# Turning the mixed input of batches 3 and 4 on VectorE, with a trip through DRAM, instead of on TensorE

## The chip, the cores and the metric

One core of a Trainium2 chip runs the whole program. The metric is the device time of one execution in microseconds; three executions of the kernel before took 647.86, 649.02 and 649.75 us (median 649.02). The engines are named as the profile names them: PE (TensorE, the matrix products; PEld is its loading of the stationary operand), DVE (VectorE), ACT (ScalarE), POOL (GpSimd) and SP (SyncE, which here only issues DMA transfers). "Line" numbers (L699) are those of the kernel before, and behind the change those of the changed kernel.

## The reference

Four batches of 768 tokens go through an attention (8 heads of 64; local window and block summaries), and its output x (768 x 512) through a mixing block:

```python
def _moe_ref(x, U, V, w_ch1, w_ch2):
    xt = x.transpose(0, 2, 1)
    h = xt @ U @ V                       # low rank mix over the tokens, rank 32
    u = x + h.transpose(0, 2, 1)         # the "mixed input"
    ch = np.maximum(u @ w_ch1, 0.0) @ w_ch2
    return (u + ch).astype(np.float32)
```

with w_ch1 of 512 x 2048 and w_ch2 of 2048 x 512. Queries and keys are drawn eight times as wide as the values.

## The kernel before, in words

Batches are numbered 1 to 4 in this text and 0 to 3 in the code (`st.b`). The program is one hand-written order of instructions for each engine; every engine works through its own in order, and waits on semaphores where an operand or a buffer isn't ready. SP's order is the DMA queue: a transfer whose source isn't ready holds those behind it.

*Stages.* Batch 1's attention comes first. Then batch 1's two large products run while batch 2's attention is slipped in between. For batches 2, 3 and 4 there is an **up phase** (u times w_ch1, by a seven-product scheme for 2 x 2 blocks, with operands B11 to T4 made ahead of it) and a **down phase** (times w_ch2). While batch b is in its two phases, batch b + 1's attention and its operands are slipped in: `later_steps` lists 32 steps and 8 calls of `operands`; the first 15 go with the up phase, the other 25 are spread evenly over the down phase, so about one for every 3.6 of its 96 output tiles. Batch 2's phases thus carry batch 3's steps, batch 3's carry batch 4's, and batch 4's carry none.

*Down phase.* For each of 16 slices f of the hidden layer there are six output tiles, four of 128 x 512 (three products each) and two of pairs of 128 x 256 (six products). The hidden values of a slice become a high part gh (ACT, L1284) and a rest gl (DVE, L1288), called a **gate** here. ACT's half for slice f + 1 is issued at the first tile of slice f, DVE's after its second. Six PSUM banks hold the output, two are left for everything else.

*Mixed input.* The attention writes x with tokens on the partitions (`st.x`, six token tiles u by 512 channels). The products want channels on the partitions. `operands(st, i, k)` does this for one channel tile c = 2i + k % 2 and one half of the tokens (hf = 1 for k = 0 and 1, else 0): `mix_u` turns three 128 x 128 blocks with an identity (L699) into a bank and adds the low rank part h in the same bank by one product (L707). From that bank ACT keeps the value in place of x (`keep`, L735, read again at the end of the batch) and makes the high part of a B operand (L738); DVE makes differences T1 to T4 with values kept earlier (L752) and the rests (L742, some on POOL). The calls are i = 0, k = 0 to 3, then i = 1, k = 0 to 3, the last four near the end of the down phase; k = 0 only keeps.

*Squares.* The attention weights of batches 3 and 4 already go a way like the new one: DVE turns 32 x 32 squares (L430), SP sends them to DRAM (L435), and fetches them sorted (L443); `value products` (L490) use them.

*Places.* `hidden_place(k)` are eight SBUF buffers h0 to h7, which hold the hidden values of slices 2k and 2k + 1 during the down phase. `val` is a ring of eight small buffers for differences, loads and outputs. `prepare` splits weights into high and low parts on ACT and POOL (L179, L180), `fetch_weight` loads them (L884).

Of the kernel before, what the change touches and what calls it, by code (L numbers as in the profile page):

```python
# [10 lines left out]
F32 = mybir.dt.float32  # L11
F32R = mybir.dt.float32r
AF = mybir.ActivationFunctionType
ALU = mybir.AluOpType
# [4 lines left out]
P = 128  # L19
BLOCK, WIN = 32, 16  # L20
NB = S // BLOCK
NU = S // P
# [12 lines left out]
NH = S // 2  # L35
# [45 lines left out]
def f32(ap):  # L81
    return ap.bitcast(F32)
# [3 lines left out]
def body(ctx: ExitStack, tc, q0, q1, k, v, vn, uv, w1, w2, mask, ident, rep, out):  # L86
    nc = tc.nc
# [10 lines left out]
    def bank(name):  # L98
        return psum.tile([P, 512], F32, name=name, tag="bank")
# [16 lines left out]
    def hidden_place(k, dt=F32):  # L116
        return wt.tile([P, 4 * NH], dt, name="place", tag=f"h{k}")
# [68 lines left out]
    def new_batch(b):  # L186
        st = Batch()
        st.b = b
        st.qt, st.kt, st.km, st.vt, st.vn, st.vsum, st.neg = ({} for _ in range(7))
        st.e, st.at, st.psx, st.t4, st.u = ({} for _ in range(5))  # L190
        st.op, st.tmp, st.h = ({} for _ in range(3))
        st.ps_s, st.ps_t, st.ps_m, st.ps_r, st.ps_u, st.ps_n = ({} for _ in range(6))
        return st

# [243 lines left out]
    def fetch_squares(st, h):  # L438
# [3 lines left out]
        for j in range(4):  # L442
            nc.sync.dma_start(  # L443
                out=at[32 * j : 32 * j + 32].rearrange("k i u q -> k i (u q)"), in_=there[j]
            )

    def turn_half(st, h, a):

        transposes(st, h, a)
        ps = st.ps_t.pop((h, a))  # L450
        if a == 0:
            st.at[h] = att.tile([P, 4, NU, 32], F32, name="at", tag=("at", "squares")[h % 2], bufs=1)
        at = st.at[h][:KC, :, 3 * a : 3 * a + 3].rearrange("k i u q -> k u i q")
        nc.scalar.copy(at, ps[:KC, : 3 * P].rearrange("k (u i q) -> k u i q", i=4, q=32))
# [86 lines left out]

    MIX, BACK = (20, 30), (22, 31)

    def later_step(st, i):

        h, a = divmod(i, 3)
        if i in PRODUCTS:  # L550
            square_values(st, PRODUCTS[i])
            normalise(st, PRODUCTS[i])
        if a == 0:
            if 1 <= h <= H:
                send_squares(st, h - 1)
            if 2 <= h <= H + 1:
                fetch_squares(st, h - 2)
            if h < H:
                scores_by_subtiles(st, h)
                exponentials(st, h, 0)  # L560
            if 3 <= h <= H:
                load_v(st, h - 1)
        elif a == 1:
            if h < H:
                exponentials(st, h, 1)
            if h + 1 < H:
                key_maxima(st, h + 1)
            if 1 <= h <= H:
                for t in range(2):
                    value_summaries(st, h - 1, t, nc.scalar.copy)  # L570
        else:
            if h + 2 < H:
                load_qk(st, h + 2)
            if h == 2:
                st.x = mo.tile([P, NU, DM], F32, name="x")
            if h < H:
                turn_squares(st, h)
        if i in (5, 8):
            load_vsum(st, 1, i // 8)
        if i in (7, 10):  # L580
            slow.append(add_vsum(st, 1, i // 10))
        if i in MIX:
            mix(st, 2 * MIX.index(i))
        if i in BACK:
            mix_back(st, 2 * BACK.index(i))
# [65 lines left out]
    def later_steps(st):  # L651

        todo = [(later_step, st, i) for i in range(STEPS)]
        for n, x in enumerate(operand_steps(st, 0)):
            todo.insert(BACK[0] + 2 + 2 * n, x)
        return todo + operand_steps(st, 1)


# [36 lines left out]
    def mix_u(st, hf, c):  # L695
# [13 lines left out]
        )  # L709
        st.ps_u[hf, c] = ps  # L710

    def mix_u_out(st, hf, c):
        if hf not in st.u:
            st.u[hf] = [
                hidden_place(4 + 2 * hf + i, F32R).rearrange("p (c q) -> p c q", q=NH) for i in range(2)
            ]
        ps = st.ps_u.pop((hf, c))
        uh, ul = st.u[hf]
        nc.scalar.copy(uh[:, c, :], ps[:, :NH])
        nc.vector.tensor_tensor(ul[:, c, :], ps[:, :NH], f32(uh)[:, c, :], ALU.subtract)  # L720


    def operands(st, i, k):

        if not st.op:
            for j, name in enumerate(OPS):
                t = wt.tile([P, 4 * NH], F32R, name="op", tag=f"op{j}")
                st.op[name] = t.rearrange("p (s i q) -> p s i q", s=2, q=NH)
        hf, c = int(k < 2), 2 * i + k % 2
        mix_u(st, hf, c)  # L730
        ps = st.ps_u.pop((hf, c))[:, :NH]
        kept = channel_rows(st, c)[:, 3 * hf : 3 * hf + 3]

        def keep():
            nc.scalar.copy(kept, ps.rearrange("p (u q) -> p u q", q=P))  # L735

        def high(name, val):
            nc.scalar.copy(st.op[name][:, 0, i], val)  # L738

        def low(name, val, engine):  # L740
            t = st.op[name][:, :, i]
            engine.tensor_tensor(t[:, 1], val, f32(t[:, 0]), ALU.subtract)  # L742

        def part(name, val):
            high(name, val)
            low(name, val, nc.gpsimd)

        def tmp():
            return mo.tile([P, DM], F32, name="tmp", tag="val", bufs=VALS)[:, :NH]

        def combine(out, a, b, op):
            nc.vector.tensor_tensor(*(by_tiles(x) for x in (out, a, b)), op)  # L752

        def by_tiles(x):
            return x if len(x.shape) == 3 else x.rearrange("p (u q) -> p u q", q=P)

        if k == 0:
            keep()
            st.tmp["B12"] = kept
            return  # L760
        name = (None, "B22", "B11", "B21")[k]
        high(name, ps)
        keep()
        if k == 1:
            st.tmp["T3"] = tmp()
            combine(st.tmp["T3"], ps, st.tmp["B12"], ALU.subtract)
            low(name, ps, nc.vector)
            part("T3", st.tmp["T3"])
        elif k == 2:
            st.tmp["T1"] = tmp()  # L770
            st.tmp["T2"] = tmp()
            combine(st.tmp["T1"], st.tmp["B12"], ps, ALU.subtract)
            combine(st.tmp["T2"], st.tmp["T3"], ps, ALU.add)
            low(name, ps, nc.vector)
            part("T1", st.tmp["T1"])
            part("T2", st.tmp["T2"])
        else:
            combine(st.tmp["T3"], ps, st.tmp["T2"], ALU.subtract)
            low(name, ps, nc.vector)
            part("T4", st.tmp["T3"])  # L780

    def channel_rows(st, c):

        return st.x[:, :, c * P : (c + 1) * P]
# [197 lines left out]
    st = sts[0]  # L982
# [117 lines left out]
    def do(items):  # L1100
        for f, *args in items:
            f(*args)
# [263 lines left out]
    for b in range(1, B):  # L1366
# [23 lines left out]
        for i, _ in enumerate(down_phase(cur, g)):  # L1390
            do(steps.get(i, ()))
            tick()
            drip()
            if after and i % NU == 0:
                do([(later_start, after, j) for j in {10: (-6,), 11: (-5,), 12: (-4,), 13: (-3, -1), 14: (-2,)}.get(i // NU, ())])
        behind = []


# [91 lines left out]
```

## Time and profile before

| | |
|---|---|
| three executions, median | 649.02 us (647.86 to 649.75) |
| the profiled execution | 648.17 us, span 646.4 us |
| granted TensorE clock | 1.000 |
| busy: PE, DVE, ACT, POOL | 97%, 56%, 55%, 56% of the span |
| DMA traffic | 115.39 MB, mean 179 GB/s |
| down phase of batch 2 (carries batch 3's steps) | about 284.5 to 369.5 us of the span |
| down phase of batch 3 (carries batch 4's steps) | about 432.7 to 517.5 us |

A row of the groups or of a line's instructions gives the engine, the operation, the tiles written and read, and how often; durations are ns of one instruction where three stand together (least, median, greatest). A row of the timeline gives the start and the length in us, and in brackets for how long the engine sat idle before and what ended that. The chain of waits is followed back from the end of the program: each row starts where the one before releases it. A stretch's row has the busy time of PE, PEld, DVE, ACT and POOL, the clock, DMA's share and GB/s. TensorE's products overlap one another, so their pace is read from starts.

### The profile page before, as it was taken

Reading aid. Unit: us, or ns where it says so; the run is one execution under the profiler, and the core shown is the slowest. Engines: PE = TensorE matmul, PEld = TensorE weight load, DVE = VectorE, ACT = ScalarE, POOL = GpSimd, SP = SyncE. Lnnn points to the kernel's source line nnn. Section 1 sums busy time; section 2 is a strip of 40 time slices with the busy share of each in tenths; the row PEclk is TensorE's granted clock in tenths of the full one; section 3 lists DMA queues with packets and bytes.
Section 4 is the critical chain, followed back from the end, with each engine's and each line's share of the span. In section 5 each row is a group of like instructions: output and inputs, shape, how many; then the busy total and the mean of one; then the engine's idle time right before and its main releaser. Section 6 shows DMA issues by size and latency. Waiting matters only on the chain.

```text
span 646.4 us, 14559 instructions
## 1 busy us (share of the span) xinstructions
PE 627.1 (97%) x5528; PEld 563.4 (87%) x5528; DVE 361.7 (56%) x1002; ACT 354.6 (55%) x788; POOL 363.3 (56%) x391
## 2 busy tenths in 40 slices
PE   5879999999999999999999999999999999999997
PEld 4669988888888899998888899998888899998886
DVE  5779767675857596566444645565544522242223
ACT  4756766656663657675453457775453455553321
POOL 3525977965766875862246765771344565653320
PEclk9999999999999999999999999999999999999999
DMA  9897588866675169896628367887431164342002
GB/s 236 223 380 222 160 296 267 229 201 189 214 232 176 46 213 290 243 265 174 180 78 218 113 204 222 258 258 203 144 116 58 60 183 142 115 131 66 32 1 99
DMA packets 68678, 115.39 MB, mean 179 GB/s; under 512 B 6912, under 2 KB 43648, under 8 KB 68608
## 3 DMA queue, kind: packets, MB, share of 16 engines
q1 hardware_dynamic: 68608, 114.45, 58.9%
q8 instruction: 44, 0.72, 0.5%
q14 instruction: 26, 0.21, 0.1%
HBM read 90.31 MB, written 24.12 MB: 177 GB/s over the span
## 4 chain that ended last, share of the span: by engine, by line
PE 87%; DMA 4%; DVE 3%; SPq 2%; ACT 2%; issue 1%; DVEq 0%; ACTq 0%
PE acc L1316 30%; PE ps_h L1215 27%; PE acc L949 10%; PE ps_h L927 9%; PE ps_x L490 3%; PE ps_s L374 2%; PE ps_s L351 2%; DMA place<-in_w 1%; PE ps_t L460 1%; SPq L215 1%; DMA kt<-in_k 1%; PE ps_u L699 1%; DMA place<-in_v 1%; DMA place<-in_q 1%; PE ps_m L665 1%
## 5 line engine op out<-in xcount | busy, mean ns | idle before, releaser
L180 POOL TENSOR_TENSOR parts<-whole,parts 128x512 fp32r<-128x512 f32 (+1 forms) x144 | 182.3, 1273 | 162.9 <-ACT parts L179 153.1
L1316 PE MATMUL acc<-gh,parts 128*128 128x256 f32 (+1 forms) x768 | 198.2, 340 | 0.0
L1215 PE MATMUL ps_h<-op,parts 128*128 128x384 f32 x1008 | 181.7, 337 | 0.1
L1215 PEld LDWEIGHTS ps_h<-op,parts 128*128 128x128 f32 x1008 | 174.3, 188 | 2.7 <-issue 1.1
L1316 PEld LDWEIGHTS acc<-gh,parts 128*128 128x128 f32 x768 | 132.9, 189 | 17.4 <-issue 1.7
L1316 PE MATMUL acc<-gl,parts 128*128 128x256 f32 (+1 forms) x384 | 129.8, 338 | 0.2
L1288 DVE SCALAR_TENSOR_TENSOR gl<-place,gh 128x768 fp32r<-128x768 f32 x48 | 55.3, 1151 | 71.3 <-ACT gh L1284 71.2
L179 ACT CAST parts<-whole 128x512 fp32r<-128x512 f32 (+1 forms) x144 | 83.3, 583 | 3.3 <-DMA whole<-up 1.0
L1316 PEld LDWEIGHTS acc<-gl,parts 128*128 128x128 f32 x384 | 72.8, 189 | 7.5 <-DVE gl L1288 0.8
L410 ACT ACTIVATE e<-e,neg 128x120 f32<-128x120 f32 x144 | 46.5, 386 | 51.4 <-DVE neg L400 46.9
L927 PE MATMUL ps_h<-place 128*128 128x384 f32 x384 | 74.3, 342 | 0.0
L1284 ACT ACTIVATE gh<-place 128x768 fp32r<-128x768 f32 x48 | 40.5, 844 | 57.1 <-PE acc L1316 48.5
L927 PEld LDWEIGHTS ps_h<-place 128*128 128x128 f32 x384 | 66.2, 188 | 1.4 <-issue 0.4
L949 PE MATMUL acc<-place,gh 128*128 128x512 f32 x192 | 67.3, 405 | 0.0
L155 POOL TENSOR_SCALAR val<-place 128x512 f32<-128x512 f32 (+1 forms) x30 | 47.7, 1607 | 25.9 <-ACT place L142 21.4
L180 POOL TENSOR_TENSOR place<-val,place 128x512 fp32r<-128x512 f32 x29 | 38.7, 1357 | 18.3 <-ACT place L179 18.3
L742 POOL TENSOR_TENSOR op<-tmp,op 128x384 fp32r<-128x384 f32 x24 | 26.3, 1108 | 32.9 <-ACT op L738 30.2
L949 PEld LDWEIGHTS acc<-place,gh 128*128 128x128 f32 x192 | 35.9, 188 | 7.6 <-POOL place L180 0.6
L400 DVE CUSTOM_DVE_ANT_0 e<-ps_s,mask_sb 128x120 f32<-128x120 f32 x144 | 32.8, 277 | 11.3 <-PE ps_s L351 5.9
L949 PE MATMUL acc<-place,gl 128*128 128x512 f32 x96 | 37.7, 393 | 0.1
L161 DVE SCALAR_TENSOR_TENSOR val<-place,val 128x512 int32<-128x512 int32 (+1 forms) x33 | 31.7, 965 | 3.3 <-POOL val L155 3.2
L1241 DVE TENSOR_TENSOR place<-place,ps_h 128x384 f32<-128x384 f32 x24 | 13.2, 551 | 36.2 <-PE ps_h L1215 36.2
(113 smaller groups left out, 796.5 us busy)
## 6 DMA issues: line engine op xcount, KB each, us to landing
place<-in_w SPq DMA_DIRECT2D x32, 512.0 KB, 5.6
whole<-up SPq DMA_DIRECT2D x24, 512.0 KB, 4.4
whole<-down SPq DMA_DIRECT2D x24, 512.0 KB, 4.3
whole<-up SPq DMA_DIRECT2D x24, 384.0 KB, 3.4
vt<-in_v SPq DMA_DIRECT2D x48, 146.2 KB, 3.8
kt<-in_k SPq DMA_DIRECT2D x24, 288.0 KB, 5.9
there<-squares SPq DMA_DIRECT2D x16, 384.0 KB, 4.3
at<-there SPq DMA_DIRECT2D x64, 96.0 KB, 3.5
```

The costliest lines, as they stand in the source:

```text
L155: nc.gpsimd.tensor_scalar(f32(bits), f32(hi), 0.0, None, ALU.mult)
L161: lambda lo, hi, bits: nc.vector.scalar_tensor_tensor(bits, lo, 29, bits, ALU.logical_shift_right, ALU.bitwise_or),
L179: nc.scalar.copy(hi, val)
L180: engine.tensor_tensor(lo, val, f32(hi), ALU.subtract)
L400: nc.vector.tensor_tensor_reduce(out=e[:, u, :], in0=ps[:, i * KC : (i + 1) * KC], in1=mask_sb[:, m, :], scale=-SCALE, scalar=BIG, op0=ALU ...
L410: nc.scalar.activation(e[:, u, :], e[:, u, :], AF.Exp, bias=st.neg[h][:, u : u + 1], scale=-1.0,)
L927: nc.tensor.matmul(ps[:, :NH], w_split[0, f][:, c % 2, part_w, c // 2], ut[:, c, :], start=(n == 0), stop=(n == 3 * NC - 1),)
L949: nc.tensor.matmul(acc[t], gt[:, sl], w_split[1, f][:, part_w], start=(first and j == 0), stop=(last and j == 2),)
L1215: nc.tensor.matmul(ps, a[:, sa, i], b[:, sb, i], start=(first and n == 0), stop=(n == 5), skip_group_check=not first,)
L1284: nc.scalar.activation(gh, h, AF.Relu)
L1288: nc.vector.scalar_tensor_tensor(gl, h, 0.0, f32(gh), ALU.max, ALU.subtract)
L1316: nc.tensor.matmul(place, w[:, part_w, c * P : (c + 1) * P], gt[:, q0:q1], start=(f == 0 and i == 0 and j == 0), stop=(f == NF - 1 and j = ...
```

## The change

For batches 3 and 4 (batch 2 keeps the old way) the three blocks are no longer turned by TensorE. For each channel tile c DVE turns all 32 x 32 squares of x's 128 x 768 values (`turn_rows`), SP sends the result to DRAM (`send_rows`, 384 KB) and fetches it in four transfers of 96 KB so that the squares stand where a full transpose has them (`fetch_rows`). The turned tiles stand in h0 and h2, the fetched ones in h1 and h3. `add_rows` then has TensorE make the low rank part alone in a bank, and DVE adds the fetched tile to it, straight into the place in x where the value is kept. ACT's copy for keeping falls away, and the high parts, differences and rests read the kept value from SBUF instead of the bank. Steps 16, 18, 25 and 29 turn tiles 0 to 3, the step behind each sends, and steps 19, 21, 28 and 31 fetch. The first four calls of `operands` stand one place later among the steps, and the first loads of batch 4 (`later_start`, in batch 2's down phase) are issued at slices 7, 9 and 11 instead of 10, 11 and 12.

```diff
--- before.py
+++ after.py
@@ -188,7 +188,7 @@
         st.b = b
         st.qt, st.kt, st.km, st.vt, st.vn, st.vsum, st.neg = ({} for _ in range(7))
         st.e, st.at, st.psx, st.t4, st.u = ({} for _ in range(5))
-        st.op, st.tmp, st.h = ({} for _ in range(3))
+        st.op, st.tmp, st.h, st.rows = ({} for _ in range(4))
         st.ps_s, st.ps_t, st.ps_m, st.ps_r, st.ps_u, st.ps_n = ({} for _ in range(6))
         return st
@@ -444,6 +444,33 @@
                 out=at[32 * j : 32 * j + 32].rearrange("k i u q -> k i (u q)"), in_=there[j]
             )
+    def turn_rows(st, c):
+        if c % 2 == 0:
+            st.turned = hidden_place(c).rearrange("p (n j u q) -> n p j u q", n=2, j=4, q=32)
+        t = st.rows[c] = st.turned[c % 2]
+        src = channel_rows(st, c).rearrange("p u (j k) -> p j u k", k=32)
+        nc.vector.transpose(t, src)
+    def send_rows(st, c):
+        there = dram.tile([P, 4, NU * 32], F32, name="rows")
+        nc.sync.dma_start(out=there, in_=st.rows[c].rearrange("p j u q -> p j (u q)"))
+        st.rows[c] = there
+    def fetch_rows(st, c):
+        if c % 2 == 0:
+            st.sorted = hidden_place(c + 1).rearrange("p (n i u q) -> n p i u q", n=2, i=4, q=32)
+        there = st.rows[c].rearrange("(i k) j c -> j k i c", k=32)
+        t = st.rows[c] = st.sorted[c % 2]
+        for j in range(4):
+            nc.sync.dma_start(
+                out=t[32 * j : 32 * j + 32].rearrange("k i u q -> k i (u q)"), in_=there[j]
+            )
     def turn_half(st, h, a):
         transposes(st, h, a)
@@ -540,6 +567,10 @@
     PRODUCTS = {9: 0, 12: 1, 14: 2, 17: 3, 20: 4, 23: 5, 26: 6, 29: 7}
     MIX, BACK = (20, 30), (22, 31)
+    ROWS = {16: 0, 18: 1, 25: 2, 29: 3}
+    FETCH = {19: 0, 21: 1, 28: 2, 31: 3}
     def later_step(st, i):
@@ -579,6 +610,11 @@
             load_vsum(st, 1, i // 8)
         if i in (7, 10):
             slow.append(add_vsum(st, 1, i // 10))
+        for behind, act in enumerate((turn_rows, send_rows)):
+            if i - behind in ROWS:
+                act(st, ROWS[i - behind])
+        if i in FETCH:
+            fetch_rows(st, FETCH[i])
         if i in MIX:
             mix(st, 2 * MIX.index(i))
         if i in BACK:
@@ -652,7 +688,7 @@
         todo = [(later_step, st, i) for i in range(STEPS)]
         for n, x in enumerate(operand_steps(st, 0)):
-            todo.insert(BACK[0] + 2 + 2 * n, x)
+            todo.insert(BACK[0] + 3 + 2 * n, x)
         return todo + operand_steps(st, 1)
@@ -709,6 +745,19 @@
         )
         st.ps_u[hf, c] = ps
+    def add_rows(st, hf, c, kept):
+        ps = bank("ps_u")
+        nc.tensor.matmul(
+            ps[:, :NH], st.t_st[:, c], vm_st[:, hf * NH : (hf + 1) * NH], start=True, stop=True
+        )
+        nc.vector.tensor_tensor(
+            kept.rearrange("p u (i q) -> p u i q", q=32),
+            ps[:, :NH].rearrange("p (u i q) -> p u i q", i=4, q=32),
+            st.rows[c][:, :, 3 * hf : 3 * hf + 3].rearrange("k i u q -> k u i q"),
+            ALU.add,
+        )
     def mix_u_out(st, hf, c):
         if hf not in st.u:
             st.u[hf] = [
@@ -727,19 +776,26 @@
                 t = wt.tile([P, 4 * NH], F32R, name="op", tag=f"op{j}")
                 st.op[name] = t.rearrange("p (s i q) -> p s i q", s=2, q=NH)
         hf, c = int(k < 2), 2 * i + k % 2
-        mix_u(st, hf, c)
-        ps = st.ps_u.pop((hf, c))[:, :NH]
         kept = channel_rows(st, c)[:, 3 * hf : 3 * hf + 3]
+        if st.b == 1:
+            mix_u(st, hf, c)
+            val = st.ps_u.pop((hf, c))[:, :NH]
+        else:
+            add_rows(st, hf, c, kept)
+            val = kept
         def keep():
-            nc.scalar.copy(kept, ps.rearrange("p (u q) -> p u q", q=P))
+            if st.b == 1:
+                nc.scalar.copy(kept, by_tiles(val))
         def high(name, val):
-            nc.scalar.copy(st.op[name][:, 0, i], val)
+            nc.scalar.copy(by_tiles(st.op[name][:, 0, i]), by_tiles(val))
         def low(name, val, engine):
             t = st.op[name][:, :, i]
-            engine.tensor_tensor(t[:, 1], val, f32(t[:, 0]), ALU.subtract)
+            engine.tensor_tensor(
+                by_tiles(t[:, 1]), by_tiles(val), by_tiles(f32(t[:, 0])), ALU.subtract
+            )
         def part(name, val):
             high(name, val)
@@ -759,24 +815,24 @@
             st.tmp["B12"] = kept
             return
         name = (None, "B22", "B11", "B21")[k]
-        high(name, ps)
+        high(name, val)
         keep()
         if k == 1:
             st.tmp["T3"] = tmp()
-            combine(st.tmp["T3"], ps, st.tmp["B12"], ALU.subtract)
-            low(name, ps, nc.vector)
+            combine(st.tmp["T3"], val, st.tmp["B12"], ALU.subtract)
+            low(name, val, nc.vector)
             part("T3", st.tmp["T3"])
         elif k == 2:
             st.tmp["T1"] = tmp()
             st.tmp["T2"] = tmp()
-            combine(st.tmp["T1"], st.tmp["B12"], ps, ALU.subtract)
-            combine(st.tmp["T2"], st.tmp["T3"], ps, ALU.add)
-            low(name, ps, nc.vector)
+            combine(st.tmp["T1"], st.tmp["B12"], val, ALU.subtract)
+            combine(st.tmp["T2"], st.tmp["T3"], val, ALU.add)
+            low(name, val, nc.vector)
             part("T1", st.tmp["T1"])
             part("T2", st.tmp["T2"])
         else:
-            combine(st.tmp["T3"], ps, st.tmp["T2"], ALU.subtract)
-            low(name, ps, nc.vector)
+            combine(st.tmp["T3"], val, st.tmp["T2"], ALU.subtract)
+            low(name, val, nc.vector)
             part("T4", st.tmp["T3"])
     def channel_rows(st, c):
@@ -1392,7 +1448,7 @@
             tick()
             drip()
             if after and i % NU == 0:
-                do([(later_start, after, j) for j in {10: (-6,), 11: (-5,), 12: (-4,), 13: (-3, -1), 14: (-2,)}.get(i // NU, ())])
+                do([(later_start, after, j) for j in {7: (-6,), 9: (-5,), 11: (-4,), 13: (-3, -1), 14: (-2,)}.get(i // NU, ())])
         behind = []
```

How the order of each engine's instructions changes is shown at three places of batch 2's down phase, near its end, where batch 3's last four calls of `operands` stand; the names are those of the code, with a buffer's number in some.

TensorE at call k = 2 (acc: the down phase's output; ps_u: the bank of the mixed input). Before:

```order
L1316 MATMUL acc_4093<-gh,parts 128x256 x2
L1316 MATMUL acc_4093<-gl,parts 128x256
L1316 MATMUL acc_4093<-gh,parts 128x256
L699 MATMUL ps_u<-ident_sb,x 128x128 x3
L707 MATMUL ps_u<-vm_st,t_st 128x384
L1316 MATMUL acc_4002<-gh,parts 128x512
L1316 MATMUL acc_4002<-gl,parts 128x512
```

And now:

```order
L1372 MATMUL acc_4095<-gh,parts 128x256 x2
L1372 MATMUL acc_4095<-gl,parts 128x256
L1372 MATMUL acc_4095<-gh,parts 128x256
L751 MATMUL ps_u<-vm_st,t_st 128x384
L1372 MATMUL acc_4002<-gh,parts 128x512
L1372 MATMUL acc_4002<-gl,parts 128x512
L1372 MATMUL acc_4002<-gh,parts 128x512
```

The three transposes are gone; the product stands at the same place.

VectorE from call k = 1 to call k = 3, with the last gate's gl between k = 2 and k = 3. Before:

```order
L752 TENSOR_TENSOR tmp<-ps_u,x 128x384
L742 TENSOR_TENSOR op<-ps_u,op 128x384
L752 TENSOR_TENSOR tmp<-x,ps_u 128x384
L752 TENSOR_TENSOR tmp<-tmp,ps_u 128x384
L742 TENSOR_TENSOR op<-ps_u,op 128x384
L1288 SCALAR_TENSOR_TENSOR gl<-place,gh 128x768
L752 TENSOR_TENSOR tmp<-ps_u,tmp 128x384
L742 TENSOR_TENSOR op<-ps_u,op 128x384
```

And now:

```order
L754 TENSOR_TENSOR x<-ps_u,place 128x3x128
L808 TENSOR_TENSOR tmp<-x 128x384
L796 TENSOR_TENSOR op<-x,op 128x384
L754 TENSOR_TENSOR x<-ps_u,place 128x3x128
L808 TENSOR_TENSOR tmp<-x 128x384
L808 TENSOR_TENSOR tmp<-tmp,x 128x384
L796 TENSOR_TENSOR op<-x,op 128x384
L1344 SCALAR_TENSOR_TENSOR gl<-place,gh 128x768
L754 TENSOR_TENSOR x<-ps_u,place 128x3x128
L808 TENSOR_TENSOR tmp<-x,tmp 128x384
L796 TENSOR_TENSOR op<-x,op 128x384
```

Each call has gained the add at its head, and the operations behind it read x in SBUF where they read ps_u.

SP from the second half of the first weights for the next up phase to the load behind it (in_vn, in_k, in_q, in_v: batch 4's first loads). Before:

```order
L884 DMA whole<-up_98 128x768
L253 DMA stage<-in_vn 128x512 x2
L201 DMA kt<-in_k 128x3x192
L215 DMA qz_84<-in_q 64x384 x2
L201 DMA kt<-in_k 128x3x192
L215 DMA qz_85<-in_q 64x384 x2
L884 DMA whole<-up_99 128x1024
```

And now:

```order
L940 DMA whole<-up_98 128x768
L470 DMA place<-rows 32x4x192 x4
L253 DMA stage<-in_vn 128x512 x2
L229 DMA vt<-in_v 96x390
L230 DMA vt<-in_v 96x390
L460 DMA rows<-place 128x768
L470 DMA place<-rows 32x4x192 x4
L940 DMA whole<-up_99 128x1024
```

The fetch of tile 2 and the trip of tile 3 now stand ahead of the load of up_99; the loads of keys and queries have moved further up.

## The prediction

> **What bounds the kernel now.** First the page: its head, the busy times, the chain of waits.
>
> ```profile
> span 646.4 us, 14559 instructions
> PE 627.1 (97%) x5528; PEld 563.4 (87%) x5528; DVE 361.7 (56%) x1002; ACT 354.6 (55%) x788; POOL 363.3 (56%) x391
> PE 87%; DMA 4%; DVE 3%; SPq 2%; ACT 2%; issue 1%; DVEq 0%; ACTq 0%
> ```
>
> TensorE (PE) sets the end. An average can hide a stage with another limit, so next the stretches (PE, PEld, DVE, ACT, POOL busy) of the two down phases that the change touches: batch 2's, in which batch 3 is prepared, and batch 3's, in which batch 4 is.
>
> ```profile
> 284.50:369.50 85.00, 84.89 (x800) 72.95 (x799) 46.16 (x113) 43.09 (x86) 40.31 (x41) 1.00 0.56 157
> 432.70:517.50 84.80, 84.75 (x798) 72.81 (x797) 43.73 (x106) 43.08 (x86) 34.21 (x29) 1.00 0.41 125
> ```
>
> TensorE has next to no gap in either, at full clock: what leaves its queue there should leave the time, unless a new wait opens. The chain, in order of time, says what its work is and where it is released by others:
>
> ```profile
> 317.75 0.33 PE ps_u L699 x3
> 318.07 0.17 PE ps_u L707
> ...
> 359.87 0.33 PE ps_u L699 x3
> 360.19 0.19 PE ps_u L707
> 360.41 0.48 ACT op L738
> 360.89 0.39 ACT x L735
> 361.36 0.56 DVE tmp L752
> 361.95 0.49 ACT op L738
> 362.83 0.85 ACT gh L1284
> 363.71 1.66 DVE gl L1288
> 365.41 4.22 PE acc L1316 x23
> ...
> 513.30 4.22 PE acc L1316 x23
> ```
>
> Each call of `operands` shows as three transposes (L699) and the product (L707). Once per phase the chain leaves TensorE: the operand step k=2 sits just ahead of the last gate (f=15), whose rounding rest gl TensorE awaits. How long it stands idle there, a row of its timeline says:
>
> ```profile
> 364.79 0.51 PE L1316 MATMUL acc<-gh,parts 128*128 128x256 f32 x2
> ```
>
> Two 256-column products start at 364.79; at 0.12 us each (half of what 512 columns take below, 0.23) the next is due at 365.03, and starts at 365.41: 0.38 us idle, once per phase.
>
> **The change, part by part.** *Removed from TensorE:* 3 transposes in each of 8 calls for two batches, 48 in 16 groups. What a group costs is the distance between starts, not the duration of one:
>
> ```profile
> 317.36 0.39 PE L1316 MATMUL acc<-gh,parts 128*128 128x512 f32 x1
> 317.59 0.49 PE L699 MATMUL ps_u<-ident_sb,x 128*128 128x128 f32 x3
> 317.83 0.42 PE L707 MATMUL ps_u<-vm_st,t_st 128*128 128x384 f32 x1
> 318.09 0.39 PE L1316 MATMUL acc<-gh,parts 128*128 128x512 f32 x1
> ```
>
> Group and product together take 318.09 − 317.59 = 0.50 us. Lower bound of the gain: first transpose to product, 0.24. Upper: the chain's 0.33, which leaves the product 0.17, its pace by columns (384 against 256 at 0.12). I take 0.33: behind a long product its weight load can be covered. 16 × 0.33 = −5.3 us (−3.8 at 0.24).
>
> *The product's wait.* It needs no turned data; it starts a bank now instead of adding to it, and the bank is freed by one VectorE add instead of after copies, differences and rests. Nothing.
>
> *Removed from ScalarE:* the 16 copies that kept the value. One of them, 0.39 us, stands in the chain above, k=2's; VectorE's add takes its place.
>
> *Added to VectorE, per phase:* four turns of 128x768, eight adds from the bank; and fourteen differences and rests that had one input in PSUM now have both in SBUF. The rows:
>
> ```profile
> L430 DVE STREAM_TRANSPOSE squares<-e x16: 964/970/974, 233.8 to 464.4; 128x768 f32<-128x768 f32 x16
> L752 DVE TENSOR_TENSOR tmp<-ps_u,x x6: 556/556/558, 160.6 to 506.6; 128x384 f32<-128x384 f32 x6
> L974 DVE TENSOR_TENSOR o<-o,place x8: 557/796/1285, 222.7 to 241.7; 128x384 f32<-128x384 f32 x8
> L1288 DVE SCALAR_TENSOR_TENSOR gl<-place,gh x48: 915/960/1990, 281.8 to 635.2; 128x768 fp32r<-128x768 f32 x48
> 295.05 0.96 DVE L1288 SCALAR_TENSOR_TENSOR gl<-place,gh 128x768 fp32r<-128x768 f32 x1 [1.10 <-ACT gh L1284]
> ```
>
> A turn costs 0.97. With a PSUM input an operation is constant (0.556 to 0.558), with two SBUF inputs of the same shape it runs from 0.56 to 1.29 (L974). So per phase 4 × 0.97 + 8 × 0.56 + 14 × 0.24 (0.80 − 0.56) = 11.7 us on 46.2 busy of 85: hidden on the average. The turn of tile 0 stands just ahead of the gate at 295.05, where VectorE idles 1.10 us anyway. An ordinary gate's gl is issued four output tiles ahead of its use, 4 × 3 × 0.23 = 2.8 us, and that covers the bursts; were it gone, each late gate would cost what it overshoots.
>
> *Where the cover is thin: the last gate.* New queue at k=2 on VectorE: add, T1, T2, rest of B11, then gl; ScalarE must do T1 and T2 before gh. From the product's end (360.38): add 0.04 + 0.56, T1 and T2, 0.04 + 0.40 for T2's high half (ScalarE's pace: 360.41 to 360.79 between copies), gh 0.04 + 0.85, gl 0.04 + 1.66: 3.63 plus T1 and T2. At 0.50 each (the pace of L1288's 0.96 halved) 4.6, at 0.80 5.2, at 1.0 (its worst, halved) 5.6. TensorE reaches the use at 365.03 − 360.38 = 4.65 now, and at 4.32 without k=3's transposes, which lie between. Idle: 0.3, 0.9 or 1.3 against 0.38, a growth of −0.1, 0.5 or 0.9; with gl at its undisturbed 0.96 instead of 1.66 the idle time vanishes, −0.4. I take 0.5, since GpSimd works throughout this place, and the differences meet it:
>
> ```profile
> 508.76 1.30 POOL L180 TENSOR_TENSOR parts<-whole,parts 128x512 fp32r<-128x512 f32 x1
> 510.43 2.00 POOL L742 TENSOR_TENSOR op<-tmp,op 128x384 fp32r<-128x384 f32 x2 [0.37 <-ACT op L738]
> 511.60 1.65 DVE L1288 SCALAR_TENSOR_TENSOR gl<-place,gh 128x768 fp32r<-128x768 f32 x1 [0.86 <-ACT gh L1284]
> 512.38 2.02 POOL L180 TENSOR_TENSOR parts<-whole,parts 128x512 fp32r<-128x512 f32 x1
> ```
>
> gl and GpSimd's L180 overlap and both are long: 1.65 for 0.96, 2.02 for 1.30. The Trainium skill (SBUF — State Buffer, Who interferes with whom) says that a VectorE instruction with two SBUF inputs and a GpSimd one that reads SBUF exclude each other, the loser waiting for the whole instruction. The trace agrees with a meeting that costs both; by the rule T1, T2 and gl could each wait out a GpSimd operation, which is the second rival's sum. Two phases: +1.0 us (−0.8 to +1.9).
>
> *Added to SP and DMA:* per phase 4 sends of 384 KB and 16 fetches of 96 KB. Tiles 0 to 2 are fetched fourteen or more output tiles ahead of their use, some 10 us. Tile 3 is the one to time:
>
> ```profile
> 298.24 1.93 SPq L443 DMA_DIRECT2D at<-there  x4
> there<-squares SPq DMA_DIRECT2D x16, 384.0 KB, 4.3
> at<-there SPq DMA_DIRECT2D x64, 96.0 KB, 3.5
> 345.13 0.56 DVE L504 TENSOR_TENSOR x<-ps_x,sum 128x384 f32<-128x384 f32 x1
> 346.66 0.34 SPq L884 DMA_DIRECT2D whole<-up  x1
> 357.06 0.50 PE L699 MATMUL ps_u<-ident_sb,x 128*128 128x128 f32 x3
> 371.10 0.62 ACT L179 CAST parts<-whole 128x512 fp32r<-128x512 f32 x1
> ```
>
> Head 7 is normalised by 345.7; turned 346.7; sent and landed 351.3; SP waits for that landing, then issues four fetches (1.9 us, as L443's four) and the last lands at 356.5. k=1's add wants it at 357.06 + 0.25 + 0.46 = 357.8. The six groups gone by then move that 2.0 us earlier, the four gone before head 7's products move the turn 1.3: spare 357.8 − 356.5 − 0.7 = 0.6 us. k=1's three operations (0.56 + 0.8 + 0.8) end 0.1 before k=2's add, some 2.3 later. Nothing taken, with 0.7 of spare. Queued behind SP's wait is the next weight load (now at 346.66, then about 353); with 4.4 us to land it is there at 358, its cast at 371.10. The moved loads of batch 4's first heads go earlier into queues that have room. Nothing.
>
> **Sum.** −5.3 + 1.0 = −4.3 us. The profiled execution took 648.17 us (1.8 around the span), and would take 643.9; the median shown is 649.02, 0.85 higher, so 644.7 is my figure. The terms' bounds: −5.3 − 0.8 = −6.1 and −3.8 + 1.9 = −1.9, that is 642.9 to 647.1.
>
> **Rivals.** *A: the last gate eats most of it.* k=1's T3 and rest already meet GpSimd's operations, so k=2's add starts late, and T1, T2, gl each wait out one (1.0 to 1.3): the growth is 1.5 to 2 us per phase. For it: gl's 1.65 above; against it: GpSimd has gaps there, such as the 0.37 us ahead of T1's low half. −5.3 + 3.5: 647.2.
>
> *B: the trip through DRAM is late and the kernel slower.* One mechanism: tile 3's fetch lands after k=1's add is due; VectorE, in order, holds k=2's chain and the last gate behind it, and TensorE stands idle. It decides from 0.7 us of lateness per phase on, one for one; a loss of 0.3% needs (4.3 + 1.9) / 2 = 3.1 more, a trip of 13.6 us instead of 9.8. For it: in batch 2's phase SP's queue holds batch 4's value loads at this place too. Against it: DMA is busy for only half of either phase (0.56 and 0.41 in the stretches). A trip 4.5 us longer: 644.7 + 2 × 3.8 = 652.3. The Trainium skill (VectorE: DVE Perf Modes, Rules for kernel authors) advises TensorE for a 128x128 turn into PSUM; no trace here compares the two whole, and the rule would be right by way of B.
>
> *C: the gap moves and no time does.* TensorE's saved time waits for something else of the stage, say weights, so the transposes were cheap filling: 649. Against it: no wait of TensorE for weights is in the chain of either phase.
>
> **Chances.** Forecast 0.66, A 0.15, B 0.10, C 0.09. Under 0.3% (1.9 us) a measurement of this kernel can't tell from none. The forecast's cases are faster but for 0.02; A 0.09 faster, 0.06 same; B 0.07 slower, 0.03 same; C 0.01 faster, 0.05 same, 0.03 slower: faster 0.74, same 0.16, slower 0.10. The range: 642.6, the sum's lower end with a little scatter, to 648.3, into A and the near side of C. The likeliest case's own is 642.9 to 647.1.
>
> **What would show it.** Right: in both down phases the distance around L707's successor about 0.17 to 0.26 instead of 0.50, the phase 2 us shorter, and one TensorE gap at gl(15) of 0.6 to 1.3 us. A: that gap above 1.8, T1 and T2 above 1 us. B: VectorE idle at k=1's add with a row fetch as releaser. C: new waits of TensorE elsewhere in the phase. Wrong beyond these: a stretch outside the two phases that changes by over a microsecond, or turned tiles that delay the square turns and so the value products.

## The result, and the profile after

| | before | changed |
|---|---|---|
| first comparison, median of 6 and 6 | 649.21 us (647.86 to 649.75) | 644.21 us (643.55 to 646.05) |
| ratio, 95% interval | | 0.9933 (0.9914 to 0.9951) |
| batch 2's down phase, batch 3's down phase | 84.09, 84.02 us | 82.68, 82.61 us |
| up phase between them, rest behind them | 63.86, 128.88 us | 63.86, 128.92 us |
| up to batch 2's down phase (these two profiles) | 285.55 us | 286.13 us |

The ratio is estimated from all executions of a comparison and isn't the quotient of the two medians (0.9923). One execution of the kernel before, 771.84 us long at a granted clock of 0.757, is left out of all comparisons.

The kernel is faster: the interval of the ratio lies below 1. But the two phases that changed give 1.41 us each, 2.8 together, and the first medians differ by 5.0: the profiled executions had 648.17 and 645.97 us, 2.2 apart, with a start that was longer by 0.58 in the changed one. What lies ahead of the phases is taken up with the experiments.

The stretches of the two phases in the kernel before, from their first product to the next up phase's (columns: PE, PEld, DVE, ACT, POOL busy with instructions, clock, DMA share, GB/s):

```profile
285.55:369.64 84.09, 83.98 (x793) 72.04 (x793) 45.83 (x111) 43.09 (x86) 39.40 (x41) 1.00 0.56 157
433.50:517.52 84.02, 83.97 (x793) 72.03 (x793) 43.53 (x105) 43.08 (x86) 33.41 (x29) 1.00 0.41 125
```

and in the changed one:

```profile
286.13:368.81 82.68, 81.37 (x769) 69.72 (x769) 52.87 (x122) 40.03 (x78) 38.51 (x39) 1.00 0.67 193
432.67:515.28 82.61, 81.37 (x770) 69.74 (x769) 51.54 (x115) 40.03 (x78) 33.29 (x29) 1.00 0.53 161
```

TensorE's busy time fell by 2.6 us in each, as its 24 fewer instructions let expect. The phase fell by 1.4: where there was a gap of 0.1 in busy time there is now one of 1.3 and 1.2. Its place, in the chain of waits of the changed kernel:

```profile
321.13 0.17 PE ps_u L751
321.31 4.89 PE acc L1372 x27
...
358.48 0.19 PE ps_u L751
358.68 0.02 issue
358.70 0.57 DVE x L754
359.27 0.03 issue
359.30 0.02 DVEq L808
359.32 0.04 issue
359.36 1.57 DVE tmp L808
360.93 0.02 issue
360.95 0.49 ACT op L792
361.45 0.07 issue
361.52 0.02 ACTq L179
361.53 0.31 issue
361.84 0.85 ACT gh L1340
362.70 0.02 issue
362.72 1.81 DVE gl L1344
364.53 0.04 issue
364.57 4.24 PE acc L1372 x23
```

The product L751 alone takes 0.17 to 0.19 where group and product took 0.50. The chain leaves TensorE at the same call k = 2 as before, by way of the add and T1, which took 1.57 us. TensorE's timeline has the gap:

```profile
362.75 0.51 PE L1372 MATMUL acc<-gh,parts 128*128 128x256 f32 x2
364.57 0.50 PE L1372 MATMUL acc<-gl,parts 128*128 128x512 f32 x1 [1.31 <-DVE gl L1344]
```

The next start was due at 362.99 and came at 364.57: 1.58 us idle from start to start (the bracket counts from the modelled end of the product before), against 0.38 in the kernel before. So per phase 8 × 0.33 = 2.64 was gained and 1.58 − 0.38 = 1.20 given back: 1.44, and 1.41 is measured.

What held T1 is seen by laying GpSimd's timeline beside VectorE's, changed kernel:

```profile
359.21 1.29 POOL L180 TENSOR_TENSOR parts<-whole,parts 128x512 fp32r<-128x512 f32 x1
359.36 1.56 DVE L808 TENSOR_TENSOR tmp<-x 128x384 f32<-128x384 f32 x1
360.85 0.55 DVE L808 TENSOR_TENSOR tmp<-tmp,x 128x384 f32<-128x384 f32 x1
361.54 2.16 POOL L796 TENSOR_TENSOR op<-tmp,op 128x384 fp32r<-128x384 f32 x2 [1.04 <-ACT op L792]
362.72 1.79 DVE L1344 SCALAR_TENSOR_TENSOR gl<-place,gh 128x768 fp32r<-128x768 f32 x1 [0.86 <-ACT gh L1340]
```

T1 began 0.15 us behind GpSimd's splitting of weights and ended 0.42 behind its end (360.50), while T2, the same kind of operation with GpSimd idle, took 0.55. The durations of that group say the same over both phases (least, median, greatest, in ns):

```profile
L808 DVE TENSOR_TENSOR tmp<-x x8: 557/558/1561, 327.2 to 505.8; 128x384 f32<-128x384 f32 x8
L754 DVE TENSOR_TENSOR x<-ps_u,place x16: 544/556/558, 321.3 to 510.9; 128x384 f32<-128x384 f32 x16
L456 DVE STREAM_TRANSPOSE place<-x x8: 970/976/982, 294.5 to 491.6; 128x768 f32<-128x768 f32 x8
```

Fourteen differences and rests in each phase read SBUF twice. Of these 28, 22 took 0.54 to 0.56 us. The other six, 0.82 to 1.56 long, had begun while a GpSimd instruction was under way, and each ended 0.41 to 0.42 behind that instruction's end. The adds, with one input in PSUM, took 0.54 to 0.56 in all 16 cases. Batch 3's phase has an add and T4's difference under one splitting of GpSimd:

```profile
510.14 2.01 POOL L180 TENSOR_TENSOR parts<-whole,parts 128x512 fp32r<-128x512 f32 x1
510.92 0.55 DVE L754 TENSOR_TENSOR x<-ps_u,place 128x384 f32<-128x384 f32 x1
511.57 1.00 DVE L808 TENSOR_TENSOR tmp<-x,tmp 128x384 f32<-128x384 f32 x1
```

The add isn't held; the difference ends at 512.57, 0.42 behind the splitting's end at 512.15. A turn took 0.98.

### The profile page after: what moved, and what is told of

It reads as the page before. It is cut to its first block, busy times and chain, and to the rows that moved or that the text cites. A ratio compares the mean times of both kernels' runs of the same rounds, so it can differ in the third digit from the quotient of the medians.

```text
span 644.2 us, 14528 instructions
## 1 busy us (share of the span) xinstructions
PE 623.3 (97%) x5480; PEld 560.6 (87%) x5480; DVE 376.6 (58%) x1026; ACT 348.2 (54%) x772; POOL 362.4 (56%) x391
## 4 chain that ended last, share of the span: by engine, by line
PE 87%; DMA 4%; DVE 4%; SPq 2%; ACT 1%; issue 1%; POOL 0%; ACTq 0%; DVEq 0%
PE acc L1372 30%; PE ps_h L1271 27%; PE acc L1005 10%; PE ps_h L983 9%; PE ps_x L517 3%; PE ps_s L374 2%; PE ps_s L351 2%; DMA place<-in_w 2%; PE ps_t L487 1%; DMA kt<-in_k 1%; SPq L215 1%; DMA place<-in_q 1%; DMA place<-in_v 1%; PE ps_m L701 1%; DVE tmp L808 1%
## 5 line engine op out<-in xcount | busy, mean ns | idle before, releaser
L1344 DVE SCALAR_TENSOR_TENSOR gl<-place,gh 128x768 fp32r<-128x768 f32 x48 | 52.8, 1101 | 60.7 <-ACT gh L1340 60.4
L179 ACT CAST parts<-whole 128x512 fp32r<-128x512 f32 (+1 forms) x144 | 83.3, 583 | 2.4 <-issue 1.1
L1297 DVE TENSOR_TENSOR place<-place,ps_h 128x384 f32<-128x384 f32 x24 | 13.2, 550 | 36.8 <-PE ps_h L1271 36.8
L1331 DVE TENSOR_TENSOR place<-place,ps_h 128x384 f32<-128x384 f32 x24 | 13.3, 554 | 35.3 <-ACT place L1330 35.2
## 6 DMA issues: line engine op xcount, KB each, us to landing
kt<-in_k SPq DMA_DIRECT2D x24, 288.0 KB, 5.3
```

The lines of the kernel that those rows point to most:

```text
L179: nc.scalar.copy(hi, val)
L1344: nc.vector.scalar_tensor_tensor(gl, h, 0.0, f32(gh), ALU.max, ALU.subtract)
```

## The experiments

Theory S: the change gives the TensorE time of the transposes, less what call k = 2's chain, longer by the add and held up by GpSimd, adds to the wait at the last gate; the trip through DRAM is hidden. Rivals are named with each run. Since phases repeat within 0.1 us from execution to execution, they are read from the profiles; ratios go with an interval.

| kernel | down phases | up phase between | ratio to before (95%) |
|---|---|---|---|
| before again | 84.07, 84.02 | 63.89 | 1.0001 (0.9982 to 1.0020) |
| changed, again | 82.68, 82.61 | 63.85 | 0.9930 (0.9911 to 0.9950) |
| changed, third time | 82.70, 82.65 | 63.85 | 0.9950 (0.9931 to 0.9970) |
| before without the transposes | 81.99, 81.82 | 63.86 | 0.9921 (0.9896 to 0.9946) |
| trip alone | 84.14, 84.07 | 63.88 | one execution |
| changed, trip of tile 3 later | 82.68, 82.61 | 63.85 | one execution |
| changed, loads moved back | 82.85, 82.61 | 63.86 | one execution |
| changed, splitting late | 81.72, 81.61 | 63.86 | 0.9917 (0.9884 to 0.9949) |
| changed, last gate first | 81.13, 81.13 | 64.60 | 0.9907 (0.9882 to 0.9932) |
| before, last gate first | 83.71, 83.70 | 63.88 | 0.9989 (0.9967 to 1.0011) |
| changed, last gate first, sums early | 81.13, 81.13 | 63.85 | 0.9907 (0.9879 to 0.9936) |

### TensorE's term alone

```diff
-        for i in range(3):
+        for i in range(3 if st.b < 2 else 0):
             nc.tensor.matmul(
...
-            ps[:, :NH], ..., start=False, stop=True
+            ps[:, :NH], ..., start=st.b > 1, stop=True
```

> The kernel before without its 48 transposes in batches 3 and 4 and with nothing in their place (their mixed input lacks x): TensorE's term alone. Theory S: eight groups of 0.33 us per phase less, the idle time at the last gate up from 0.38 by the one group between call k = 2 and the gate: 84.05 - 2.62 + 0.33 = 81.75 per phase, -4.6 us in all. Rival (the transposes are cheap filling, 0.24 us a group): -1.92 + 0.24, 82.4 per phase, -3.4.

Measured 81.99 and 81.82, 2.10 and 2.20 us less than before; 81.75 was expected, and 82.4 by the rival. The gap at the last gate in this kernel's timeline:

```profile
360.50 0.51 PE L1316 MATMUL acc<-gh,parts 128*128 128x256 f32 x2
361.63 0.50 PE L1316 MATMUL acc<-gl,parts 128*128 128x512 f32 x1 [0.62 <-DVE gl L1288]
```

Due at 360.74, it came at 361.63: 0.89, against 0.38 + 0.33 expected. With that gap read off, 84.09 − 2.64 + 0.51 = 81.96, where the rival's 0.24 a group would leave 82.68. The term of 0.33 holds, and the wait at the gate takes part of it back even with nothing put in the transposes' place: 0.33 because call k = 3's no longer lie between, and some 0.2 more, with a splitting of weights on ScalarE (L179, 0.52 us) now in the chain just ahead of k = 2's first copy.

### The trip alone

The changed kernel with the old `mix_u` for all batches: turns, sends and fetches are made, and nobody reads the fetched tiles.

```diff
-        if st.b == 1:
-            mix_u(st, hf, c)
-            val = st.ps_u.pop((hf, c))[:, :NH]
-        else:
-            add_rows(st, hf, c, kept)
-            val = kept
+        mix_u(st, hf, c)
+        val = st.ps_u.pop((hf, c))[:, :NH]
...
-            if st.b == 1:
-                nc.scalar.copy(kept, by_tiles(val))
+            nc.scalar.copy(kept, by_tiles(val))
```

> The kernel before with the turns on VectorE, the sends and the fetches and the new places of steps and loads, whose result isn't used: the mixed input is still turned by TensorE. The price of the trip alone. Theory S: hidden, phases of 84.1 and 84.0 within 0.1 us. Rival (VectorE's turns or the traffic hold something back): a phase longer by 0.5 us or more, or a new wait of TensorE in it.

Each phase is 0.05 longer than before: the trip is hidden. Four turns, four sends and 16 fetches cost a phase at most 0.1 us. That a fetch isn't late can't be seen here, since nobody reads it; in the changed kernel call k = 1's add started at 356.40 without a wait in its row.

### Call k = 2 behind the last gate

```diff
         steps = spread(theirs, 0, DOWN - 5)
+        if ahead:
+            steps[85] = steps.pop(83)
```

> The changed kernel with call k = 2 of the last four moved two output tiles back, behind the last gate. Theory S (TensorE's 1.58 us gap ahead of that gate's rest, one per phase, is k = 2's chain on VectorE and ScalarE ahead of the gate): no gap, each phase 82.64 - 1.58 = 81.1, 3.2 us less than the changed kernel. Rival (the wait only moves: B11 and B21 are then late for the next up phase): the gap is gone but the next up phase, 63.86 us now, grows by as much, and the total stays.

Both phases are 81.13: the gap is gone and with it 1.55 and 1.48 us. The rival has its part, too: the up phase behind batch 2's down phase grew by 0.74. Its timeline shows the wait, and who ends it:

```profile
374.14 2.18 PE L1271 MATMUL ps_h<-op,parts 128*128 128x384 f32 x11 [0.48 <-POOL parts L180]
```

It isn't B11 or B21, as the rival had it, but a splitting of weights that GpSimd reaches late, behind T1's and T2's rests and batch 4's value sums. Behind batch 3's down phase, where there are no such sums, the rest of the program keeps its length.

The same move in the kernel before:

> The kernel before (transposes on TensorE) with call k = 2 moved behind the last gate and nothing else. Theory S: its idle time there is 0.38 us a phase, so 83.7 per phase, -0.8 us in all, which a measurement can't tell from none: of the gap at the last gate only 0.38 belonged to the kernel before, the other 1.2 came with the change. Rival (the move pays by itself as much as in the changed kernel): 82.5 per phase, -3.2.

Down phases of 83.71 and 83.70, as theory S had it: the kernel before had 0.4 to win there, the other 1.2 of the changed kernel's gap came with the change.

### Is it GpSimd that holds T1?

The changed kernel, with the splitting that T1 met issued behind call k = 2's work:

```diff
-            if seen[f] == 3:
+            if seen[f] == (6 if f == NF - 3 and st.b < B - 1 else 3):
                 prepare()
```

> The changed kernel with one splitting of weights (ScalarE's high part, GpSimd's rest) issued behind call k = 2's work instead of two output tiles ahead of it. Theory S with the lock (T1 took 1.56 us because it waited for the end of GpSimd's 1.29 us of that splitting): T1 0.56, the gap 1.58 - 1.0 = 0.6, each phase 81.6. Rival (T1 is slow because both its inputs lie in SBUF, whoever else works): T1 stays at 1.5, the phase at 82.6.

VectorE's and GpSimd's timelines of this kernel:

```profile
359.77 0.56 DVE L808 TENSOR_TENSOR tmp<-x 128x384 f32<-128x384 f32 x1
360.25 0.55 DVE L808 TENSOR_TENSOR tmp<-tmp,x 128x384 f32<-128x384 f32 x1
360.96 2.16 POOL L796 TENSOR_TENSOR op<-tmp,op 128x384 fp32r<-128x384 f32 x2 [1.29 <-ACT op L792]
362.65 1.29 DVE L1344 SCALAR_TENSOR_TENSOR gl<-place,gh 128x768 fp32r<-128x768 f32 x1 [1.38 <-ACT gh L1340]
```

T1 takes 0.56 with GpSimd out of the way, and the phases are 0.96 and 1.00 shorter than in the changed kernel. So both inputs in SBUF are not slow by themselves; the meeting is. The size came out as expected, but by another way. ScalarE's half of the moved splitting now stands ahead of the gate's gh, as the chain of this kernel shows:

```profile
361.26 0.62 ACT parts L179
361.87 0.76 ACT gh L1340
```

That takes back about half of T1's 1.0: gl begins 3.57 us behind the end of k = 2's product, where it was 4.05. The other half is gl itself, 1.29 instead of 1.79.

That the loser waits out the winner's whole instruction, as the Trainium skill states it (SBUF — State Buffer, Who interferes with whom), agrees with T1's 1.56, which ended 0.42 behind GpSimd's instruction, a little less than T1's own length. The other five meetings of the changed kernel ended at the same distance.

### How close is tile 3's trip?

```diff
-    ROWS = {16: 0, 18: 1, 25: 2, 29: 3}
+    ROWS = {16: 0, 18: 1, 25: 2, 30: 3}
```

> The changed kernel with tile 3 turned one step (four output tiles, 3.8 us) later. In the changed kernel its last fetch is issued at 351.3 and call k = 1's add starts at 356.40 without waiting for it. Theory from that trace: the fetch lands at about 357.7, the add waits 1.3 us, and 0.6 us of gap in VectorE's queue ahead of k = 2 takes half of it: each phase 0.5 to 1.0 us longer, 83.2 to 83.7. By the prediction's own spare of 0.7 us: 3.8 - 0.7 = 3.1 us longer, 85.8. If the trip doesn't bind even so: 82.6.

Nothing changed: 82.68 and 82.61, and the expectation was a miss. VectorE and SP of this kernel show why:

```profile
347.96 0.96 DVE L456 STREAM_TRANSPOSE place<-x 128x768 f32<-128x768 f32 x1
348.95 0.34 SPq L460 DMA_DIRECT2D rows<-place  x1
351.28 1.75 SPq L470 DMA_DIRECT2D place<-rows  x4
357.46 0.56 DVE L754 TENSOR_TENSOR x<-ps_u,place 128x384 f32<-128x384 f32 x1
```

A step later in the order was only about 2 us later in time, since VectorE isn't held to TensorE's pace there: the turn moved behind one gate's gl and no further. The send was read back 2.3 us after it was issued, and all four fetches were out by 353.0; the transfers of rows in this stretch land in 2.0 to 3.6 us, so by 356.6 at the latest, and the add at 357.46 came no later against its product than before. The trip has spare time that this run didn't use up; where it begins to bind wasn't reached.

### The moved loads

```diff
-                ... {7: (-6,), 9: (-5,), 11: (-4,), 13: (-3, -1), 14: (-2,)} ...
+                ... {10: (-6,), 11: (-5,), 12: (-4,), 13: (-3, -1), 14: (-2,)} ...
```

> The changed kernel with batch 4's first loads back at slices 10, 11 and 12 of batch 2's down phase. Prediction's step: the moved loads cost and bring nothing, 82.68 for that phase. Rival: left where they were, they stand in SP's queue and the DMA engines around tile 3's trip, its fetch lands after call k = 1's add is due, and batch 2's down phase (not batch 3's, which has no such loads) grows by 0.5 us or more.

Batch 2's down phase is 0.17 longer, batch 3's the same. The loads do stand in the way of tile 3's trip, whose fetches are issued at 352.00 instead of 349.56:

```profile
352.00 1.74 SPq L470 DMA_DIRECT2D place<-rows  x4
356.51 0.56 DVE L754 TENSOR_TENSOR x<-ps_u,place 128x384 f32<-128x384 f32 x1 [0.19 <-issue]
359.72 1.64 DVE L808 TENSOR_TENSOR tmp<-tmp,x 128x384 f32<-128x384 f32 x1
```

Counted from the phase's start, k = 1's add comes 0.45 us later than in the changed kernel. Of that, 0.34 is there already when the gl ahead of it begins, behind copies for batch 4's keys on VectorE (L333) that took 1.11 for 0.77. The rest fits the last fetch, issued at 353.3, with 3.0 us for the slowest of the four; the profile names no releaser for the 0.19. Then T1 (0.77), T2 (1.64) and the rest of B11 (1.37) each meet a GpSimd instruction. The rival had the direction and a third of the size; its mechanism is at most a part of it.

### The start

> The changed kernel unchanged, timed again. Theory S (the two down phases carry all of it: 84.09 and 84.02 us became 82.68 and 82.61, so -2.8 us, and the rest of the first median's -5.0 is the start, which differs between executions of the same kernel): two phases of 82.6 again, the median over many runs nearer to -2.8 than to -5. Rival R (the change shortens something outside the phases by about 2 us, too): -5 again, and the stretch up to batch 2's down phase shorter than the 285.55 us of before.

> The kernel before, unchanged, timed as the others are, for the stretch ahead of batch 2's down phase (285.55 us before; 286.13, 284.19, 285.63, 283.90 and 286.54 in the profiles of the change and its variants, though nothing in that stretch differs). Theory (that stretch differs between executions, by the first loads): a ratio whose interval holds 1, phases of 84.1, 63.9 and 84.0 as before. Rival (the kernel before has a longer start than its variants): still a ratio of 1, since both sides have it; then the profile's start would lie at 285.5 or above.

> The changed kernel once more. Both earlier comparisons gave 0.993, where the phases alone (2.8 us of 648) give 0.9957, just outside both intervals; the other variants' ratios fit their phases. If the stretch ahead of the phases differs by chance, this comparison should fall nearer to 0.9957 and the starts (span less 358.0) spread over 283 to 287.5 with a median near 285.5, as those of the kernel before do. If the changed kernel has a shorter start for a reason of its own: 0.993 a third time, and a median start near 284.2.

In the second comparison the changed kernel had 643.82 us against 648.16, in the third 645.20 against 648.37. The kernel before against itself gives 1.0001. The phases come out the same each time. The stretch ahead of them, taken as the span less what follows it, ranges over 282.8 to 288.0 us in 61 executions of the kernel before (mean 285.5) and over 282.8 to 286.5 in 21 of the changed one (mean 284.7), with one order of each engine's operations in both. Two profiles of the same changed kernel differ in it by 1.94 us (286.13 and 284.19), and have that difference and more when batch 1's first product of the down part begins (56.62 and 53.44); the chain of the first comparison's profile and that of the second one's:

```profile
31.06 9.80 DMA place<-in_w
40.88 6.96 DMA kt<-in_k
56.62 2.11 PE acc L1005 x8
```

```profile
27.43 6.50 DMA place<-in_v
53.44 2.12 PE acc L1005 x8
```

In the one, loads of weights and keys are waited for until 47.84; in the other they are not in the chain. So in these two the first loads make the difference. They aren't the whole of it: in the kernel before, profiled again, that product begins at 56.40 without those loads in its chain, and what else moves the start stays open. Of the three ratios 0.9933, 0.9930 and 0.9950, the first two leave 0.9957, the phases' 2.8 us, just outside their intervals, the third holds it, and the nine starts of the third spread from 282.8 to 286.5 with a median of 285.4, as was expected for chance. But over all runs the mean start of the changed kernel is 0.8 us shorter, with standard deviations of 1.1 and 1.4, which makes a standard error of 0.3. Whether that 0.8 is chance isn't settled; nothing in the two kernels' order accounts for it.

### A better version

The last gate first, and batch 4's value sums where GpSimd was idle:

```diff
+        if ahead:
+            steps[85] = steps.pop(83)
...
-                ... {7: (-6,), 9: (-5,), 11: (-4,), 13: (-3, -1), 14: (-2,)} ...
+                ... {7: (-6,), 9: (-5,), 11: (-4,), 12: (-2,), 13: (-3, -1)} ...
```

> The changed kernel with call k = 2 behind the last gate, and with the value sums of batch 4's first heads (GpSimd) begun at slice 12 of batch 2's down phase instead of 14. In the run with the call moved alone the up phase behind batch 2's down phase took 64.60 us instead of 63.86, waiting for a splitting on GpSimd that stood behind these sums. Theory: GpSimd is idle for 4.8 us between slices 12 and 14, the sums fit there, the up phase takes 63.86 again and each down phase 81.1; 5.8 us less than before over the phases. Rival (GpSimd is short of time through the whole end of the phase): the up phase stays at 64.6.

Down phases of 81.13, up phase 63.85, as expected. The median was 641.92 us against 648.10, the ratio 0.9907 (0.9879 to 0.9936); by the phases it is 5.9 us below the kernel before and 3.0 below the change.

## Why the prediction was right, and where it wasn't

- **The forecast.** 644.7 was forecast and 644.21 measured, with a range of 642.6 to 648.3. The time was met better than its working, and that is luck: the sum said −4.3 and the phases gave −2.8, inside the bounds of −1.9 to −6.1; the rest of the first difference lies in the start, which the prediction took as equal and which isn't from run to run. From the median of 649.02 the phases alone lead to 646.2.
- **TensorE's term** (0.33 a group, 5.3 in all): right. The product's successor starts 0.17 to 0.19 later, the upper bound was the true one, and the run without transposes accounts for it within 0.03 us with its gap read off.
- **The wait at the last gate** is the step that was mis-sized: growth of 0.5 per phase (bounds −0.4 to 0.9) against 1.20. The mechanism, the place and the reader of the wait were as said; TensorE was due 4.32 us behind the product's end (362.99 − 358.67), as worked out. The chain was too short: T1 and T2 took 2.04 for 1.6, the step from add to T1 0.09 that was left out, gl 1.81 for 1.66. The prediction averaged a row (L974, 0.80) that GpSimd's timeline takes apart: seven of its eight operations began under a GpSimd instruction and ended 0.41 to 0.42 behind that one's end, and the eighth, with GpSimd idle, took 0.56. The splitting that T1 met was there, too. Rows of the kernel before show one of the meetings of L974, and that splitting:

```profile
231.72 1.29 POOL L180 TENSOR_TENSOR parts<-whole,parts 128x512 fp32r<-128x512 f32 x1 [0.63 <-ACT parts L179]
232.15 1.28 DVE L974 TENSOR_TENSOR o<-o,place 128x384 f32<-128x384 f32 x1
360.88 1.30 POOL L180 TENSOR_TENSOR parts<-whole,parts 128x512 fp32r<-128x512 f32 x1
```

  That splitting begins 0.50 behind the product's end (360.38) and T1 was due at 0.60, so it would end at 0.50 + 1.30 + 0.42 = 2.22. That is an estimate of 1.6 for T1, and 1.56 was measured; an average can't say it.
- **Rival A** (1.5 to 2 per phase, T1, T2 and gl each waiting one out) had the right mechanism and too many meetings: call k = 1's T3 and rest took 0.56 each and held nothing up, T1 and gl met GpSimd, T2 didn't. The truth lay between: the gap of 1.58 misses the 0.6 to 1.3 named as the sign of the forecast, and stays under A's 1.8; the phase lost 1.41 and not 2.
- **VectorE's added work**: 11.7 us per phase was worked out, 7.0 and 8.0 were added. The turns and adds took 8.3 for 8.4. Only three of the 14 two-input operations in each phase met GpSimd, 1.9 and 2.0 us for the 3.4 put down, and the 15 gl took 1.2 and 1.3 less in all, which the working had left as they were; copies and outputs account for most of what remains. Hidden, as said.
- **The trip** (rival B): landing of tile 3's last fetch was put at 356.5, with 0.7 of spare (0.6 in its sum). In the changed kernel the send was read back 3.5 us after its issue, and the last fetch, issued at 350.9, had at most 3.5 to land (2.3 in the median of the four), so it was there by 354.4; medians over the whole program, 4.3 and 3.5, were too slow for this place. A trip 1.9 us later cost nothing. B didn't occur.
- **Rival C** (no time moves) fell with the phases, and with the run that only leaves the transposes out.
- **The moved loads** were called free; put back they cost 0.17 in one phase. Right in size, though tile 3's fetches were issued 2.4 us later with the loads back. The weight load behind SP's wait came at 351.41 instead of 346.66, and nobody waited for it.

## What to carry to other kernels

Taking work off the bounding engine is worth the distance between starts that it held, here 0.11 us a transpose and not the 0.27 that one lasts in the trace (L699, mean); and it brings every later deadline nearer by as much, so look first at what that engine waited for by a few tenths already. When work moves to VectorE, operations that read PSUM and now read SBUF twice are no longer free of GpSimd: price them by what is under way at that moment, here 0.56 with nothing, or up to 0.42 behind the end of the GpSimd instruction, and not by the mean. A chain that feeds the next phase did better here behind the last gate of this one than ahead of it.

## What the runs showed of the hardware that was not expected

The first product of batch 1's down part begins anywhere from 53.4 to 56.6 us in three profiles of the changed kernel, while its phases of 83 us repeat within 0.04; a change of half a percent in this kernel is better read from phases than from totals. And a VectorE operation with two SBUF inputs, alone, took the same 0.56 us as one with a PSUM input; what looked like a slower source in the mean (0.80) was only the GpSimd instruction under way, whose end it outlasted by 0.41 to 0.42 us each time.
